# Filler matmuls in front of the last two weighted sums, and three quarters of tile 14's spread on VectorE

## The chip, the core and the metric

The kernel runs on one core of one Trainium2 chip. The metric is the device time in microseconds of one execution; the time before is the median of three runs, 365.45 us (365.2 to 366.1). A core has TensorE for matrix products, VectorE (DVE), ScalarE (ACT) and GpSimd (POOL) for elementwise work, and SyncE (SP), which here issues nearly all DMAs. Each engine takes its instructions in the order in which the program lists them; engines wait for each other by semaphores.

## The reference

One step of decoding for a batch of 8, with a gate `g` per row between attention and a small MLP:

```
g = sigmoid(sum(x * gate_w))                      # x: 8 x 576
q = x @ wq                                        # 32 heads of 128, 16 key/value heads
p = softmax(q . k * 128**-0.5)                    # the last 2048 positions of each cache
a = (p . v) @ wo                                  # wo: 4096 x 576
b = gelu(layernorm(x) @ w1 + b1) @ w2 + b2        # w1: 576 x 4608
out = g * a + (1 - g) * b
```

Everything is bf16. The key and value caches, 64 MB each in the part used, are nearly all of the 154 MB that are read.

## The kernel before, in words

The caches are cut into 16 K tiles and 16 V tiles of 4 MB, each for 32 pairs of batch row and head and a quarter of the positions. They stream through four slots of the arena (`RAW`), one DMA each, in the order K0 K1 V0 K2 V1 ... K15 V14 V15, then the bias b2, two pieces of w2 (`M` 0), the four blocks of wo (`W`) and the last three pieces of w2 (`M` 1). A DMA is issued by SyncE as soon as what used its slot is done; V14's slot takes the last block of wo and the last pieces of w2, so those wait for the weighted sum of tile 14.

For each tile n:

- VectorE transposes the K tile in four parts into the KT area (`tr`, L693), TensorE makes the scores (`qk`, L711, of which all but the first of four matmuls keep the loaded weights and are recorded in the helper at L175).
- VectorE takes the running maximum (`mx`, L644), ScalarE the exponentials (`exp`, L650) into P, VectorE transposes P (`pt`, L668).
- The P tile is spread into a block layout, a quarter (32 partitions x 2048) per instruction (`qrx`, L743 on VectorE and GpSimd, L742 on ScalarE). `px_engs` (L615) names the engine of each quarter: GpSimd two and ScalarE two, for tiles 0 to 13; one GpSimd, one ScalarE, two VectorE for tile 14; one ScalarE, three VectorE for tile 15.
- TensorE makes the weighted sum of V (`pv`, 64 matmuls of 128x256). Sums 0 to 14 are looped: two matmuls from L756, five rounds of twelve with register addresses (helper at L186), two more. Sum 15 is unrolled in two parts of 48 and 16 (`pva`, `pv`).
- VectorE adds the sum to the group's result (`o`, L792 and L794).

The block layout holds zeros between its blocks. Tiles 0 to 14 use the area `PX`, cleared once at the start (`ptx0`, L606). Tile 15 uses the KT area, which GpSimd clears by a memset of 128x4096 fp32 (`ktx0`, L726) after the last score matmuls; the spreads of tile 15 wait for it.

After sum 15, VectorE, GpSimd and TensorE bring the result into place (L794, L797, L800, L802, L805), ScalarE and VectorE into bf16 columns (L808, L809), and TensorE adds up the output: bias and w2 blocks, then wo (`proj0` to `proj3`), then the last w2 blocks, all at L580. Between the wo blocks and the last w2 blocks stand fillers (`keep_warm`, L814): matmuls of zeros that nobody reads, five (`warm0`) before `proj3`, five (`warm1`) after it. The first of a group is recorded at L819, the others at L175.

The order on each engine is no queue of the chip: a planner (`_Plan.schedule`, L62) places each operation by an assumed cost, a priority, its dependences (`deps`) and an order (`after`). Only `deps` become semaphore waits; `after` merely keeps an operation from being placed before another has been. Before, `ktx0` stands `after` the GpSimd quarter of tile 14 (L747), and the maximum of tile 15 `after` tile 14's VectorE quarters (L748).

Of the kernel before, what the change touches and what calls it, by code (L numbers as in the profile page):

```python
# [170 lines left out]
ARENA_BASE = 16512  # L171
# [21 lines left out]
def build_kernel(nc, A_x, A_k_cache, A_v_cache, A_wq, A_wo, B_x, B_w1, B_b1, B_w2, B_b2, gate_w, out):  # L193
# [10 lines left out]
    NL = 4 * NG  # L204
# [17 lines left out]
    with ExitStack() as es:  # L222
# [365 lines left out]
        for vi in range(NL):  # L588
            stream.append(("V", vi))
            if vi + 2 < NL:  # L590
                stream.append(("K", vi + 2))
        HEAD, BODY, TAIL = 2, 12, 2
        ROUNDS = (64 - HEAD - TAIL) // BODY
        assert HEAD and TAIL and HEAD + ROUNDS * BODY + TAIL == 64
        held_regs = []

        def regs():
# [14 lines left out]
        grp_done, acc_done = {}, {}  # L612
        mask_done, mx_done = {}, {}
        grp_first, sums = {}, {}
        px_engs = [("pool", "pool", "act", "act")] * (NL - 2) + [("pool", "act", "dve", "dve"), ("act", "dve", "dve", "dve")]  # L615

        def take_slot():
            n = n_slot[0]
# [109 lines left out]
        def v_item(n):  # L728
            s, d = load_item(A_v_cache, "dv", n)
            g, i = divmod(n, 4)  # L730
            if n == NL - 1:
                spread(n)
            ob_ = BK_OS[n % 2]
            px_at = aoffs("KT") if n == NL - 1 else PX
            px_free = [o_kz] if n == NL - 1 else [pv_done.get(n - 1), o_px0]
            px_done[n] = []
            for c in range(4):
                def fn(e, c=c):
                    dst = bass.AP(arena, offset=32 * c * AST + px_at + 32 * c, ap=[[AST, 32], [128, 64], [1, 32]])
                    src = bass.AP(arena, offset=32 * c * AST + aoffs("PT") + 2048 * (n % 2), ap=[[AST, 32], [32, 64], [1, 32]])  # L740
                    if px_engs[n][c] == "act":
                        return e.activation(out=dst, in_=src, func=ACTF.Copy)  # L742
                    return e.tensor_copy(dst, src)  # L743
                px_done[n].append(add(px_engs[n][c], fn, deps=[pt_done[n]] + px_free, name="qrx%d_%d" % (n, c), cost={"act": 1.8, "dve": 0.8, "pool": 2.4}[px_engs[n][c]], prio=5))

            if n == NL - 2:
                o_kz.after.append(px_done[n][0])  # L747
                mx_done[n + 1].after.extend(op for op in px_done[n] if op.eng == "dve")  # L748

            def pv_part(a, b):  # L750
                def fn(e):
                    mm = None
                    for k in range(a, b):
                        lhsT = bass.AP(arena, offset=px_at + 128 * k, ap=[[AST, 128], [1, 128]])
                        rhs = bass.AP(arena, offset=aoffs("RAW") + s * DE + 128 * k, ap=[[AST, 128], [SE, 2], [1, 128]])
                        mm = e.matmul(ps[:, ob_, 0:256], lhsT, rhs, start=(k == 0), stop=True, skip_group_check=True)  # L756
                    return mm
                return fn

            def pv_fn(e):  # L760
                pv_part(0, HEAD)(e)
                l, r = regs()
                e.reg_mov(l[0], ARENA_BASE + 2 * (PX + 128 * HEAD) + 254)
                e.reg_mov(r[0], ARENA_BASE + 2 * (aoffs("RAW") + s * DE + 128 * HEAD))
                with e.Fori(0, ROUNDS):
                    for i in range(BODY):
                        if i % 3 == 0:
                            if i:
                                e.reg_add(l[0], l[0], 768)
                                e.reg_add(r[0], r[0], 768)  # L770
                            for k in range(1, min(3, BODY - i)):
                                e.reg_add(l[k], l[0], 256 * k)
                                e.reg_add(r[k], r[0], 256 * k)
                        reg_matmul(nc, e, ps[:, ob_, 0:256], l[i % 3], [[AST, 128], [1, 128]], r[i % 3], [[AST, 128], [SE, 2], [1, 128]])
                    step = 256 * (BODY - (BODY - 1) // 3 * 3)
                    e.reg_add(l[0], l[0], step)
                    e.reg_add(r[0], r[0], step)
                return pv_part(64 - TAIL, 64)(e)
            deps = [d, o_u] + px_done[n] + [o_done.get(n - 2)]
            after = pv_hist[-1:] + [qk_unit.get(n + 1)]  # L780
            if n < NL - 1:
                pv = add("pe", pv_fn, deps=deps, name="pv%d" % n, cost=8.2, after=after)
            else:
                pva = add("pe", pv_part(0, 48), deps=deps, name="pv%da" % n, cost=5.4, after=after)
                sums[g].after.append(pva)
                pv = add("pe", pv_part(48, 64), deps=deps, name="pv%d" % n, cost=1.8, after=[sums[g]])
            pv_hist.append(pv)
            pv_done[n] = pv
            slot_free[s] = [pv]
            al = sm[:, n, 3:4]  # L790
            if i == 0:
                o_done[n] = add("dve", lambda e: e.tensor_copy(Oc, ps[:, ob_, 0:256]), deps=[pv, acc_done.get(g - 1)], name="o%d" % n, cost=0.4, prio=6)  # L792
            else:
                o_done[n] = add("dve", lambda e: e.scalar_tensor_tensor(out=Oc, in0=Oc, scalar=al, in1=ps[:, ob_, 0:256], op0=ALU.mult, op1=ALU.add), deps=[pv, al_done[n], o_done[n - 1]], name="o%d" % n, cost=0.5, prio=6)  # L794
            if i == 3:
                vmv = vm.rearrange("p (r d) -> p r d", r=2)
                vmul = add("dve", lambda e: e.scalar_tensor_tensor(out=vmv, in0=Oc.rearrange("p (r d) -> p r d", r=2), scalar=sg[:, g, 4:5],  # L797
                                                                   in1=bass.AP(arena_f, offset=foffs("maskrh"), ap=[[AST // 2, 128], [1, 2], [0, 128]]), op0=ALU.mult, op1=ALU.mult),
                           deps=[o_done[n], o_maskrh, o_hf] + grp_done[g], name="vmul%d" % g, cost=0.5, prio=6)
                acc_done[g] = add("dve", lambda e: e.tensor_reduce(out=EV, in_=vm.rearrange("p (r d) -> p d r", r=2), axis=AXL.X, op=ALU.add),  # L800
                                  deps=[vmul, us_done.get(g - 1)], name="acc%d" % g, cost=0.6, prio=6)
                ew = add("pool", lambda e: e.tensor_tensor(out=EW, in0=bass.AP(arena_f, offset=foffs("EV"), ap=[[AST // 2, 128], [0, 2], [1, 128]]),  # L802
                                                           in1=bass.AP(arena_f, offset=foffs("maskhd"), ap=[[AST // 2, 128], [1, 2], [0, 128]]), op=ALU.mult),
                         deps=[acc_done[g], o_maskhd, us_done.get(g - 1)], name="ew%d" % g, cost=0.6, prio=6)
                us_done[g] = add("pe", lambda e: e.matmul(ps[:, BK_S, 256:512], selv[:, 6 - 2 * g:134 - 2 * g], EW.rearrange("p h d -> p (h d)"), start=(g == 0), stop=True, skip_group_check=True),  # L805
                                 deps=[ew, o_u] + o_selv, name="us%d" % g, cost=0.7, prio=6)
            if n == NL - 1:
                oev = add("act", lambda e: e.activation(out=on, in_=ps[:, BK_S, 256:512], func=ACTF.Copy, scale=gcol), deps=[us_done[NG - 1], o_gcol], name="oev", cost=0.45, prio=9)  # L808
                o_T.append(add("dve", lambda e: e.transpose(bass.AP(arena, offset=aoffs("oT"), ap=[[AST, 128], [1, 256]]),  # L809
                                                            bass.AP(arena, offset=aoffs("on"), ap=[[AST, 128], [1, WOR], [WOR, 32]])), deps=[oev], name="oT", cost=0.6, prio=9))  # L810

        us_done, o_T = {}, []

        def keep_warm(name, n, after):  # L814
            def fn(e):
                mm = None
                for k in range(n):
                    args = (ps[:, k % 4, :], zeros_bf, maskR)
                    mm = e.matmul(*args, start=True, stop=True, skip_group_check=True) if k == 0 else held_matmul(nc, e, *args, start=True, stop=True, skip=True)  # L819
                return mm  # L820
            return add("pe", fn, deps=[ex_done[NL - 1], o_z, o_mR], name=name, cost=0.22 * n, after=after)

        def wo_all(_):
            def place(s, at, i):
# [6 lines left out]
                return AccGroup("proj%d" % i, [(oT[:, j, i, :], dj[:, j, :]) for j in range(WOR)], o_T + [d], cost=1.0, prio=1).op  # L831
            s = take_slot()
            done = [place(s, WO_CH * D * i, i) for i in range(3)]
            warm = keep_warm("warm0", 5, done[2:])
            slot_free[s] = done
            s = take_slot()
            done = [place(s, 0, 3)]
            done[0].after.append(warm)
            o_m2.append(keep_warm("warm1", 5, done))
            m2_at.append((s, WO_CH * D))  # L840
            slot_free[s] = done

# [104 lines left out]
```

## Time and profile before

| what | value |
|---|---|
| median of 3 runs (lowest, highest) | 365.45 us (365.2, 366.1) |
| the profiled execution's own time | 365.17 us |
| its span, first to last instruction | 363.9 us |
| TensorE, VectorE, ScalarE, GpSimd busy | 76%, 70%, 36%, 22% of the span |
| DMA | 154.47 MB, mean 424 GB/s |
| granted TensorE clock, mean | 0.93 |

The span is what the trace covers; the profiled execution took 1.3 us more. Times in the trace are counted from the span's start. "Granted clock" is the share of TensorE's full clock that it was given. A row of the timeline gives start and length, engine, line, operation, what is written and read and, in brackets, how long the engine was idle before and what ended that. TensorE has two rows, PE for matmuls and PEld for loads of weights. Since a line may be that of a helper, matmuls of several operations share L175 and L186.

### The profile page before, as it was taken

The page shows a single profiled execution, that of the slowest core. Times are in us where ns is not written, and L with a number is a line of the kernel's source. Part 1 is how long each engine was busy: PE and PEld are TensorE (multiplying, and loading weights), DVE is VectorE, ACT ScalarE, POOL GpSimd, SP SyncE. Part 2 cuts the span into 40 slices and gives each one's busy share as a digit, 9 for nine tenths or more (in the row PEclk, how much of TensorE's full clock was granted, in tenths as well). Part 3 has the DMA queues.
Part 4 walks back from the last instruction along what each step waited for, and adds up shares of the span by engine and source line. Part 5 has one row for each costly group of instructions (what it writes and reads, how often), then busy time and mean ns, then how long its engine had stood idle before and what let it go on. Part 6 is the DMA issues. An engine that isn't in the chain of part 4 may idle for free.

```text
span 363.9 us, 4246 instructions
## 1 busy us (share of the span) xinstructions
PE 277.4 (76%) x1818; PEld 126.9 (35%) x1381; DVE 254.9 (70%) x195; ACT 131.6 (36%) x117; POOL 78.8 (22%) x77
## 2 busy tenths in 40 slices
PE   0356464999897958996978769786868789975997
PEld 0110000345171704361434316251606043612863
DVE  0722978797978596949496878767685969398520
ACT  1012106274544442634343334444444417303400
POOL 9124001230414040402212040404040404006000
PEclk9976596999998998999899989999999879998999
DMA  8999999999999999999999999999999999999995
GB/s 348 433 439 402 461 403 458 407 457 418 447 420 443 421 443 425 434 430 432 436 432 436 432 430 432 443 421 447 418 447 416 450 414 451 414 450 413 420 428 226
DMA packets 6579, 154.47 MB, mean 424 GB/s; under 512 B 764, under 2 KB 932, under 8 KB 1320
## 3 DMA queue, kind: packets, MB, share of 16 engines
q1 hardware_dynamic: 6512, 154.29, 98.5%
q8 instruction: 7, 0.11, 0.1%
q10 hardware_dynamic: 56, 0.03, 0.0%
q14 instruction: 4, 0.03, 0.0%
HBM read 154.31 MB, written 0.01 MB: 424 GB/s over the span
## 4 chain that ended last, share of the span: by engine, by line
DMA 45%; DVE 35%; PE 13%; issue 4%; ACT 2%; POOL 0%; ACTq 0%
DMA arena<-in_A_k_cache_dram 43%; DVE arena L693 20%; DVE arena L668 5%; PE ps L175 4%; PE ps L186 2%; PE ps L756 2%; DMA arena<-in_gate_w_dram 2%; PE ps L580 2%; DVE arena L644 2%; DVE arena L797 1%; PE ps L502 1%; DVE arena L794 1%; DVE arena L743 1%; PE ps L711 1%; DVE arena L563 1%
## 5 line engine op out<-in xcount | busy, mean ns | idle before, releaser
L693 DVE STREAM_TRANSPOSE arena<-arena 128x2048 f32<-128x2048 f32 x64 | 145.0, 2288 | 28.4 <-DMA arena<-in_A_k_cache_dram 26.8
L175 PE MATMUL ps<-arena 128*128 128x512 bf16 (+2 forms) x446 | 126.8, 432 | 11.6 <-DVE arena L693 8.3
L743 POOL COPY arena<-arena 32x2048 bf16<-32x2048 bf16 x29 | 55.1, 1902 | 227.1 <-DVE arena L668 212.2
L186 PE MATMUL ps<-arena 128*128 x900 | 102.3, 275 | 0.0
L186 PEld LDWEIGHTS ps<-arena 128*128 x900 | 88.9, 99 | 11.3 <-issue 0.3
L711 PE MATMUL ps<-arena 128*128 128x512 bf16 x121 | 50.5, 417 | 50.1 <-DVE arena L693 43.4
L742 ACT ACTIVATE arena<-arena 32x2048 bf16<-32x2048 bf16 x30 | 57.2, 1906 | 70.5 <-DVE arena L668 67.8
L650 ACT ACTIVATE arena<-ps,arena 128x2048 bf16<-128x2048 f32 x16 | 31.5, 1967 | 107.6 <-DVE arena L648 74.7
L711 PEld LDWEIGHTS ps<-arena 128*128 128x128 bf16 x128 | 13.2, 103 | 162.5 <-DVE arena L693 104.7
L644 DVE TENSOR_REDUCE arena<-ps 128x1 f32<-128x2048 f32 x16 | 36.7, 2292 | 32.8 <-PE ps L175 32.8
L668 DVE STREAM_TRANSPOSE arena<-arena 128x2048 bf16<-128x2048 bf16 x16 | 36.4, 2274 | 2.1 <-ACT arena L650 2.1
L654 ACT ACTIVATE ps<-arena 128x2048 f32<-128x2048 f32 x15 | 28.1, 1872 | 0.1
L756 PE MATMUL ps<-arena 128*128 128x256 bf16 x124 | 19.0, 275 | 3.8 <-DVE arena L743 3.7
L756 PEld LDWEIGHTS ps<-arena 128*128 128x128 bf16 x124 | 12.0, 99 | 17.0 <-issue 14.0
L453 PE MATMUL ps<-arena 8*128 8x8 bf16 x8 | 0.6, 171 | 14.8 <-DVE arena L427 9.6
L558 DVE TENSOR_TENSOR arena<-arena 128x1152 f32<-128x1152 f32 x1 | 1.4, 1358 | 11.4 <-ACT arena L556 11.4
L580 PE MATMUL ps<-arena 128*8 128x288 bf16 (+1 forms) x140 | 9.3, 286 | 0.0
L637 POOL COPY arena<-arena 32x128 bf16<-32x128 bf16 x16 | 4.6, 287 | 15.3 <-ACT arena L537 7.7
L580 PEld LDWEIGHTS ps<-arena 128*8 128x8 bf16 (+1 forms) x140 | 5.8, 86 | 4.9 <-issue 1.9
L427 DVE COPY arena<-arena 8x64 bf16<-8x64 bf16 x2 | 0.3, 190 | 9.2 <-DMA arena<-in_gate_w_dram 9.2
L794 DVE SCALAR_TENSOR_TENSOR arena<-arena,ps 128x256 f32<-128x256 f32 x12 | 5.4, 447 | 1.4 <-PE ps L756 1.4
L890 DVE CAST arena<-ps 8x288 bf16<-8x288 f32 x1 | 0.4, 445 | 8.4 <-PE ps L580 8.4
(104 smaller groups left out, 99.0 us busy)
## 6 DMA issues: line engine op xcount, KB each, us to landing
arena<-in_A_k_cache_dram SPq DMA_DIRECT2D x16, 4096.0 KB, 27.1
arena<-in_A_v_cache_dram SPq DMA_DIRECT2D x16, 4096.0 KB, 26.9
arena<-in_B_w_dram SPq DMA_DIRECT2D x1, 4608.0 KB, 23.4
arena<-in_A_wo_dram SPq DMA_DIRECT2D x4, 1152.0 KB, 22.5
arena<-in_A_wq_dram SPq DMA_DIRECT2D x1, 4096.0 KB, 13.0
arena<-in_B_w_dram SPq DMA_DIRECT2D x2, 1728.0 KB, 24.3
arena<-in_B_w_dram SPq DMA_DIRECT2D x1, 1152.0 KB, 17.4
arena<-in_B_w_dram SPq DMA_DIRECT2D x1, 576.0 KB, 24.3
```

The source lines that it names most:

```text
L175: return e.add_instruction(mybir.InstMatmult(name=nc.get_next_instruction_name(), engine=mybir.EngineType.PE, ins=[e.lower_ap(rhs), e.lowe ...
L186: return e.add_instruction(mybir.InstMatmult(name=nc.get_next_instruction_name(), engine=mybir.EngineType.PE, ins=[operand(r, r_ap), opera ...
L580: ins = e.matmul(ps[32 * j:32 * j + 8, BK_ACC, 0:JN], lhsT, rhs[:, JN * j:JN * j + JN], start=False, stop=True, skip_group_check=True, til ...
L644: mx = mx_done[n] = add("dve", lambda e: e.tensor_reduce(out=k(n, MX), in_=ps[:, 0:4, :].rearrange("p a n -> p (a n)"), axis=AXL.X, op=ALU ...
L650: ex = add("act", lambda e: e.activation(out=Pm, in_=ps[:, 0:4, :].rearrange("p a n -> p (a n)"), func=ACTF.Exp, bias=k(n, NB), scale=SCAL ...
L654: mask_done[n + 1] = add("act", lambda e: e.activation(out=ps[:, 0:4, :].rearrange("p a (n c) -> p (a n) c", c=32), in_=bass.AP(arena_f, o ...
L668: pt_done[n] = add("dve", lambda e: e.transpose(bass.AP(arena, offset=aoffs("PT") + 2048 * (n % 2), ap=[[AST, 128], [1, 2048]]), Pm), deps ...
L693: tr = add("dve", (lambda rh=rh, hh=hh, kb=kb: lambda e: e.transpose(bass.AP(arena_f, offset=foffs("KT") + kb * 2048, ap=[[AST // 2, 128], ...
L711: mm = e.matmul(*args, start=False, stop=True, skip_group_check=True) if rc == 0 else held_matmul(nc, e, *args, stop=True, skip=True)
L742: return e.activation(out=dst, in_=src, func=ACTF.Copy)
L743: return e.tensor_copy(dst, src)
L756: mm = e.matmul(ps[:, ob_, 0:256], lhsT, rhs, start=(k == 0), stop=True, skip_group_check=True)
```

## The change

The spread of tile 14 moves from one GpSimd, one ScalarE, two VectorE quarters to one ScalarE, three VectorE. With it goes the order of `ktx0` behind the first quarter. The fillers `warm0` go, `warm1` has three matmuls where it had five; new fillers, ten before sum 14 and six before sum 15, stand behind whatever is ahead of those sums on TensorE. They write the PSUM bank of the sum that follows, after the sum of two tiles before has been read from it. Sums 0 to 13 are looped in ten rounds of six instead of five of twelve; sum 14 keeps twelve; the first 48 matmuls of sum 15 are looped in three rounds of fourteen. VectorE's addition of sum 14 is placed after VectorE's quarters of tile 15.

```diff
-        HEAD, BODY, TAIL = 2, 12, 2
-        ROUNDS = (64 - HEAD - TAIL) // BODY
-        assert HEAD and TAIL and HEAD + ROUNDS * BODY + TAIL == 64
+        HEAD = 2
...
-        px_engs = [("pool", "pool", "act", "act")] * (NL - 2) + [("pool", "act", "dve", "dve"), ("act", "dve", "dve", "dve")]
+        px_engs = [("pool", "pool", "act", "act")] * (NL - 2) + [("act", "dve", "dve", "dve"), ("act", "dve", "dve", "dve")]
...
             if n == NL - 2:
-                o_kz.after.append(px_done[n][0])
                 mx_done[n + 1].after.extend(op for op in px_done[n] if op.eng == "dve")
...
-            def pv_fn(e):
+            def pv_looped(e, end, tail, body):
                 pv_part(0, HEAD)(e)
...
-                with e.Fori(0, ROUNDS):
-                    for i in range(BODY):
+                with e.Fori(0, (end - HEAD - tail) // body):
+                    for i in range(body):
...
-                return pv_part(64 - TAIL, 64)(e)
+                return pv_part(end - tail, end)(e)
             deps = [d, o_u] + px_done[n] + [o_done.get(n - 2)]
             after = pv_hist[-1:] + [qk_unit.get(n + 1)]
+            if n >= NL - 2:
+                after.append(keep_warm("warm_pv%d" % n, (10, 6)[n - NL], after, (ob_,), [o_u, o_done[n - 2]]))
             if n < NL - 1:
-                pv = add("pe", pv_fn, deps=deps, name="pv%d" % n, cost=8.2, after=after)
+                pv = add("pe", lambda e: pv_looped(e, 64, 2, 6 if n < NL - 2 else 12), deps=deps, name="pv%d" % n, cost=8.2, after=after)
             else:
-                pva = add("pe", pv_part(0, 48), deps=deps, name="pv%da" % n, cost=5.4, after=after)
+                pva = add("pe", lambda e: pv_looped(e, 48, 4, 14), deps=deps, name="pv%da" % n, cost=5.4, after=after)
...
             al = sm[:, n, 3:4]
+            if n == NL - 1:
+                o_done[n - 1].after.extend(op for op in px_done[n] if op.eng == "dve")
...
-        def keep_warm(name, n, after):
+        def keep_warm(name, n, after, banks=(0, 1, 2, 3), deps=None):
             def fn(e):
                 mm = None
                 for k in range(n):
-                    args = (ps[:, k % 4, :], zeros_bf, maskR)
+                    args = (ps[:, banks[k % len(banks)], :], zeros_bf, maskR)
...
-            return add("pe", fn, deps=[ex_done[NL - 1], o_z, o_mR], name=name, cost=0.22 * n, after=after)
+            return add("pe", fn, deps=[o_z, o_mR] + (deps or [ex_done[NL - 1]]), name=name, cost=0.22 * n, after=after)
...
-            warm = keep_warm("warm0", 5, done[2:])
...
-            done[0].after.append(warm)
-            o_m2.append(keep_warm("warm1", 5, done))
+            o_m2.append(keep_warm("warm1", 3, done))
```

## The prediction, made before the changed kernel ran

> **What bounds the kernel now.** I read the page first. Its second part shows the DMA row at 9 tenths in every slice but the first and the last, and part 3 gives the hardware queue 98.5% of the 16 engines' span: 154 MB at 424 GB/s set the pace until about 10 us before the end. Then I read the chain of work that ended last, in order of time, to see where the pace passes to the engines.
>
> ```profile
> 293.03 25.41 DMA arena<-in_A_k_cache_dram
> 318.46 6.61 DVE arena L693 x3
> ...
> 327.71 2.23 DVE arena L668
> 329.97 0.68 DVE arena L743
> 330.65 0.03 issue
> 330.69 2.28 DVE arena L743
> 332.97 0.14 issue
> 333.10 0.41 PE ps L756 x2
> ```
>
> Columns are start, length, engine, line. The last K tile lands, VectorE transposes it (L693) and the P tile of sum 14 (L668), spreads two quarters of it (L743), and TensorE starts the weighted sum of tile 14 at 333.10. From there the chain is 8.9 us of that sum (333.10 to 342.00), sum 15 (342.21 to 349.5), the normalisation through VectorE, GpSimd and TensorE (to 352.4), and output blocks up to 361.97. The DMA issues page gives the other limit: the last three w2 pieces are issued from 342.40 to 343.4 and land 17.4 to 18.0 us later, the last at about 343.4 + 17.8 = 361.2. So at the end two limits lie less than 1 us apart: shortening the engines' chain can win at most some 0.6 us, and lengthening it costs in full.
>
> The two spreads above look alike and are not: 0.68 and 2.28 us for the same 32x2048 copy. The timeline shows what lay beside them.
>
> ```profile
> 329.97 2.98 DVE L743 COPY arena<-arena 32x2048 bf16<-32x2048 bf16 x2
> ...
> 330.00 2.40 POOL L743 COPY arena<-arena 32x2048 bf16<-32x2048 bf16 x1 [20.62 <-DVE arena L668]
> 332.52 3.88 POOL L726 MEMSET arena<- 128x4096 f32 x1
> ```
>
> GpSimd's copy ends at 332.40, VectorE's second copy 0.57 later: it stood still while GpSimd worked. In its turn GpSimd's copy took 2.40 where the other 28 took about 1.89: it waited for VectorE's first copy. The memset of L726 took 3.88; VectorE's copy ended 0.45 after the memset's start, and the rest is 3.43. Three copies with GpSimd idle, at 339.94, took 2.12 together.
>
> **Part 1: GpSimd no longer spreads a quarter of tile 14; VectorE takes three.** Alone this would be a gain: 2.12 instead of 3.00 us, so VectorE would be free at 332.1, not 332.97. But the same edit drops the ordering that put the memset of the KT area (L726, `ktx0`) behind that quarter on GpSimd's queue. What is left is its dependence on the last score matmuls, which end at 329.39 (L175, 328.55 + 0.84). GpSimd has nothing else queued, and in the memset of L606 it started 0.07 after TensorE's last matmul (32.80 to 32.87). So the memset starts at about 329.5, half a microsecond before VectorE's copies are ready at 329.97. What a VectorE instruction does when it meets a running memset is shown once:
>
> ```profile
> 32.87 3.51 POOL L606 MEMSET arena<- 128x4096 f32 x1 [5.24 <-PE ps L175]
> ...
> 35.40 1.59 DVE L559 TENSOR_SCALAR arena<-arena 128x1152 f32<-128x1152 f32 x1
> ```
>
> The memset ends at 36.38; the tensor_scalar begins inside it and ends at 36.99, 0.61 later, and took longer than the two-input operations of the same size (L558 and L560, 1.36). I read it as held back until the memset was over. Then the memset runs 329.5 to 333.0, the first copy ends 0.6 later, the other two take 1.4: VectorE is done at **335.0, not 332.97: 2.0 us late**. If nothing blocked, it would be 332.1 (0.9 early); these are the ends.
>
> The Trainium skill, SBUF — State Buffer, section Who interferes with whom, says that a VectorE copy in a two-port mode and a GpSimd instruction take one shared port pair by turns, whichever starts first keeping it for the whole instruction; the rows here agree (0.57 and 0.61 us after GpSimd's end). If the two shared the port instead, the copies would creep at the 0.68 : 2.28 ratio until 333.0 and end near 334.2, and the sum below would be 0.8 smaller.
>
> ScalarE's quarter (329.97, 1.91 us) is untouched. Behind the three copies on VectorE's queue stands the maximum of tile 15 (L644), and behind it the whole of tile 15: from 332.97 to the end of its spreads at 342.06 are 9.1 us, none of which changes (its spreads already were one on ScalarE and three on VectorE). So tile 15 is ready at 335.0 + 9.1 = **344.1**.
>
> **Part 2: fillers before the two sums.** Ten 128x512 matmuls on TensorE behind the last score unit: 0.225 each by the pace of L175 (0.84 for three, ends overlapping), 2.25 us, 329.45 to 331.7. They lie in TensorE's wait and cost nothing; their own waits, tile 12's evacuation at 307.79 and memsets of the start, are long over. What they should save is the clock. The granted clock in stretches of 3.41 us (columns: stretch, length, PE busy, PEld, DVE, ACT and POOL busy with counts, clock, DMA share, GB/s):
>
> ```profile
> 111.45:114.87 3.42, 1.44 (x7) 0.19 (x2) 3.42 (x5) 3.01 (x2) 2.95 (x2) 1.00 1.05 450
> 114.87:118.28 3.41, 3.18 (x10) 0.53 (x3) 2.14 (x4) 1.09 (x2) 0.82 (x1) 0.50 1.07 461
> 265.05:268.47 3.42, 1.50 (x7) 0.10 (x1) 3.42 (x2) 1.72 (x1) 1.69 (x1) 1.00 1.02 441
> 268.47:271.88 3.41, 2.19 (x10) 0.41 (x5) 3.13 (x5) 2.38 (x3) 2.08 (x2) 1.00 1.07 461
> 329.91:333.32 3.41, 0.22 (x2) 0.13 (x2) 3.31 (x4) 1.91 (x1) 3.20 (x2) 1.00 0.91 394
> 333.32:336.73 3.41, 3.41 (x18) 2.32 (x17) 2.12 (x2) 1.22 (x1) 3.09 (x1) 0.50 0.96 404
> ```
>
> With 1.44 of 3.42 us busy the next stretch runs at half clock, with 1.50 it does not: idle of some 1.95 us inside one stretch is the limit. Before, the gap was 3.7 us (329.39 to 333.10) and sum 14 paid: 8.9 us against 7.14 for sum 13 (312.26 to 319.40), 1.76. After, the copies hold sum 14 until 335.0 + 0.13 = 335.1, so the gap behind the fillers is 335.1 - 331.7 = 3.4 us. Wherever the stretches fall, one holds over 1.95 us of it except when it is split nearly in half (both parts between 1.45 and 1.95: 0.5 of 3.41, 15%). The loss is 1.7 when the whole half-clock stretch falls on the sum and about 0.9 when it begins in the gap; I take 1.5. Sum 14 then ends at 335.1 + 7.14 + 1.5 = 343.75 (342.25 without the loss).
>
> Six fillers before sum 15 are queued behind sum 14 and the small group matmul (0.2 us, as 342.00 to 342.21): 6 x 0.225 = 1.35. Sum 15 starts at 343.75 + 0.2 + 1.35 = **345.3**, later than its tile's 344.1: the fillers are now on the path. Before it started at 342.21, so **+3.1** (ends: +2.0, where tile 15 sets it, and +3.4).
>
> **Part 3: loops.** Sums 0 to 13 go in rounds of six, five more branches each. Sixty looped matmuls took 6.71 us (112 ns each) and 48 unrolled ones 5.40 (112.5), so the branches of today cost nothing seen. Upper end: one TensorE issue wait of 0.29 (333.49) per new branch, 1.5 us per sum; even then sum 13 would end at 320.9, against 320.83 for the next score unit, and K loads are issued 27 us before they land. I take 0. Sum 15's first 48 become looped: 0, at most 0.2 either way.
>
> **Part 4: fillers after.** `warm0` and two of `warm1` go.
>
> ```profile
> 352.37 4.58 PE L580 MATMUL ps<-arena 128*8 128x288 bf16 x72
> ...
> 358.06 1.15 PE L580 MATMUL ps<-arena 128*8 128x288 bf16 x16
> ...
> 359.14 0.39 PE L819 MATMUL ps<-arena 128*128 128x512 bf16 x1
> ...
> 360.33 1.64 PE L580 MATMUL ps<-arena 128*8 128x288 bf16 x24
> ```
>
> `warm0` took 356.95 to 358.06, 1.11; two of `warm1` are 0.45. **-1.56**, all on the path if TensorE is late. The block of wo rows behind it is issued at 342.03 and landed 14.9 later, 356.9; after the change its issue follows sum 14 to about 343.8, with 1.1 MB blocks issued at 327.4 still landing 22.5 us later in front of it, so the queue doesn't run dry.
>
> **Sum:** +3.1 - 1.56 = +1.55; TensorE ends at 363.5, past the landing at 361.2. The profiled execution took 365.17 (span 363.9 and 1.3 around it): 366.7. The median of the runs shown, 365.45, is 0.28 above it; I say **366.8**, range of this case 366.0 to 367.3.
>
> **Rivals.** (1) The copies are blocked but the clock holds: +2.0 - 1.56, 365.6 to 365.9. For it the 15% split; against it the gaps of 1.98 us (114.05) and 2.41 us (172.27) that cost the clock. The Trainium skill, TensorE: Matmul & The Clock Gate, section What's actually happening, asks for an idle window of about 3.4 us; by that this rival would be the rule, but 111.45:114.87 lost the clock with 1.44 us of work in it. 0.13. (2) On the other side: VectorE's copies aren't blocked, because the memset only writes or starts after them. Spreads end at 332.1, the gap is 0.5 us, the clock holds, sum 14 runs 332.2 to 339.35, tile 15 is ready at 341.2 and sum 15 starts 0.95 earlier; then wo (356.9) and the last w2 pieces (360.9 and 361.2) bind and TensorE ends near 361.4: -0.55, 364.6 to 364.9. No change is a start of sum 15 at 342.21 + 1.56 = 343.8: copies that end at 334.6 with the clock held (344.1 came from 335.0), at 333.5 with 1.5 lost. Before that point it isn't slower. Against it L559 and the 2.28 us copy. 0.11. (3) The new branches show after all, or the order of the end shifts: over 367.4, 0.04. The forecast: 0.72.
>
> A measurement of this kernel can't tell under 0.3% from no change. That puts the line at 366.55: of the forecast's 0.72 some 0.48 lie above it. Slower 0.52, the same 0.42, faster 0.06. Range 364.7 to 367.4.
>
> **What would show it.** The memset of L726 at 329.5, VectorE's three copies taking over 4 us from 329.97, sum 14 starting near 335.1 at half clock, six fillers directly in front of sum 15, no wait for w2 at the end. Wrong if the copies take 2.1 us beside the memset, or if the last matmuls wait for a DMA.

## The result, and the profile after

The changed kernel takes 366.51 us (median of 7 runs, 366.12 to 366.92); the kernel before took 365.22 beside it (365.19 to 366.1). The ratio of the two, as measured side by side, is 1.0029 with a 95% interval of 1.0017 to 1.0041 (the quotient of the medians would be 1.0035): slower than no change, by about 0.3%, and the interval doesn't say on which side of 0.3% it lies. The profiled execution took 366.66 us, its span is 365.4.

The timeline of the kernel after shows GpSimd's memset (now L724) and VectorE's three quarters of tile 14 (now L741):

```profile
329.47 3.51 POOL L724 MEMSET arena<- 128x4096 f32 x1 [20.05 <-PE ps L175]
...
329.99 4.96 DVE L741 COPY arena<-arena 32x2048 bf16<-32x2048 bf16 x3
```

The memset starts half a microsecond ahead and ends at 332.98. The three copies take 4.96 us; the same three for tile 15 take 2.12 (341.94). The chain of waits splits them and goes on to sum 15:

```profile
329.99 3.53 DVE arena L741
...
333.55 0.69 DVE arena L741
...
335.10 0.38 PE ps L753 x2
335.50 8.39 PE ps L186 x60
343.89 0.22 PE ps L753 x2
344.10 0.12 PE ps L672 x2
344.22 0.24 PE ps L821
344.46 1.08 PE ps L175 x5
345.54 0.22 PE ps L753 x2
```

Only the first copy is long (the next takes 0.69), and it ends at 333.52, 0.54 after the memset: nearly all of its work, 0.69 us where nothing is beside it, came after GpSimd had ended. Sum 14 starts at 335.10 and lasts until 344.1; a small matmul (L672) and the six fillers (L821, L175), to 345.4, stand on the chain, directly in front of sum 15. The stretches of 3.41 us around it (PE busy, PEld, DVE, ACT, POOL, granted clock, DMA share, GB/s):

```profile
333.01:336.42 3.41, 1.30 (x11) 0.97 (x12) 3.32 (x4) 0.00 (x0) 0.00 (x0) 1.00 0.99 426
336.42:339.83 3.41, 3.41 (x19) 2.35 (x17) 1.25 (x3) 2.29 (x4) 0.00 (x0) 0.50 0.97 415
339.83:343.24 3.41, 3.41 (x33) 3.05 (x32) 3.34 (x3) 1.64 (x2) 0.00 (x0) 1.00 0.99 422
```

The stretch with the end of the gap has 1.30 us of work, and all of the next runs at half clock: 19 matmuls where the one behind it has 33. The end, from the timeline:

```profile
355.55 5.56 PE L580 MATMUL ps<-arena 128*8 128x288 bf16 x88
...
361.79 1.64 PE L580 MATMUL ps<-arena 128*8 128x288 bf16 x24
```

The last wo block follows the others without a pause (88 matmuls in one row) and nothing waits for a DMA. TensorE ends at 363.43, 1.46 later than before.

### The profile page after: what moved, and what is told of

Its sections match the earlier page's. It is cut to its first block, busy times and chain, and to the rows that moved or that the text cites. A ratio compares the mean times of both kernels' runs of the same rounds, so it can differ in the third digit from the quotient of the medians.

```text
span 365.4 us, 4420 instructions
## 1 busy us (share of the span) xinstructions
PE 276.6 (76%) x1829; PEld 126.8 (35%) x1382; DVE 256.7 (70%) x196; ACT 131.6 (36%) x117; POOL 76.1 (21%) x76
## 4 chain that ended last, share of the span: by engine, by line
DMA 45%; DVE 35%; PE 13%; issue 4%; ACT 2%; POOL 0%; ACTq 0%
DMA arena<-in_A_k_cache_dram 43%; DVE arena L691 20%; DVE arena L666 5%; PE ps L175 4%; PE ps L186 4%; DMA arena<-in_gate_w_dram 2%; PE ps L580 2%; DVE arena L642 2%; DVE arena L799 1%; DVE arena L741 1%; PE ps L502 1%; DVE arena L796 1%; PE ps L753 1%; PE ps L709 1%; DVE arena L563 1%
## 5 line engine op out<-in xcount | busy, mean ns | idle before, releaser
L175 PE MATMUL ps<-arena 128*128 128x512 bf16 (+2 forms) x457 | 127.4, 427 | 11.7 <-DVE arena L691 8.7
L186 PE MATMUL ps<-arena 128*128 x942 | 107.1, 275 | 0.0
L186 PEld LDWEIGHTS ps<-arena 128*128 x942 | 92.8, 99 | 11.9 <-issue 0.3
L741 POOL COPY arena<-arena 32x2048 bf16<-32x2048 bf16 x28 | 52.8, 1885 | 206.7 <-DVE arena L666 205.9
L709 PE MATMUL ps<-arena 128*128 128x512 bf16 x120 | 49.3, 411 | 52.6 <-DVE arena L691 45.9
L648 ACT ACTIVATE arena<-ps,arena 128x2048 bf16<-128x2048 f32 x16 | 31.5, 1968 | 108.4 <-DVE arena L646 75.5
L709 PEld LDWEIGHTS ps<-arena 128*128 128x128 bf16 x128 | 13.1, 102 | 163.7 <-DVE arena L691 107.4
L642 DVE TENSOR_REDUCE arena<-ps 128x1 f32<-128x2048 f32 x16 | 36.7, 2291 | 31.8 <-PE ps L175 31.7
L753 PE MATMUL ps<-arena 128*128 128x256 bf16 x82 | 14.3, 272 | 3.5 <-DVE arena L741 3.5
L753 PEld LDWEIGHTS ps<-arena 128*128 128x128 bf16 x82 | 8.0, 99 | 18.6 <-issue 16.1
L635 POOL COPY arena<-arena 32x128 bf16<-32x128 bf16 x16 | 4.6, 287 | 15.3 <-ACT arena L537 7.7
L724 POOL MEMSET arena<- 128x4096 f32 x1 | 3.5, 3511 | 20.0 <-PE ps L175 20.0
L804 POOL TENSOR_TENSOR arena<-arena 128x256 f32<-128x256 f32 x4 | 2.5, 613 | 23.7 <-DVE arena L802 23.7
L741 DVE COPY arena<-arena 32x2048 bf16<-32x2048 bf16 x6 | 7.0, 1160 | 0.2
## 6 DMA issues: line engine op xcount, KB each, us to landing
arena<-in_B_w_dram SPq DMA_DIRECT2D x1, 1152.0 KB, 15.3
```

The costliest lines, as they stand in the source:

```text
L175: return e.add_instruction(mybir.InstMatmult(name=nc.get_next_instruction_name(), engine=mybir.EngineType.PE, ins=[e.lower_ap(rhs), e.lowe ...
L186: return e.add_instruction(mybir.InstMatmult(name=nc.get_next_instruction_name(), engine=mybir.EngineType.PE, ins=[operand(r, r_ap), opera ...
L642: mx = mx_done[n] = add("dve", lambda e: e.tensor_reduce(out=k(n, MX), in_=ps[:, 0:4, :].rearrange("p a n -> p (a n)"), axis=AXL.X, op=ALU ...
L648: ex = add("act", lambda e: e.activation(out=Pm, in_=ps[:, 0:4, :].rearrange("p a n -> p (a n)"), func=ACTF.Exp, bias=k(n, NB), scale=SCAL ...
L709: mm = e.matmul(*args, start=False, stop=True, skip_group_check=True) if rc == 0 else held_matmul(nc, e, *args, stop=True, skip=True)
```

## The experiments

Each ran beside the kernel before on the same chip, and its ratio is to that: e1 to e4 on one chip (median of before 365.49 us), e5 to e8 on another (365.21). In the traces of e1 to e5 the last K tile's transposes begin 0.3 to 0.4 us later than in the kernel before (318.8 to 318.9, not 318.5), so times inside those are compared from VectorE's first copy or from the start of sum 14, not from the span's start. A sum of V is timed from the start of its first matmul to the end of its last.

**e1: the memset behind the copies.**

```diff
             if n == NL - 2:
+                o_kz.deps.extend(px_done[n])
```

> The changed kernel, with one wait more: the memset of the KT area (ktx0) waits for all four quarters of tile 14's spread, so it can't run beside them. Theory (the running memset holds VectorE's copies back): the three copies take 2.1 us and end at 332.1, sum 14 starts at 332.2 after a gap of about 0.6 us on TensorE, at full clock, and ends near 339.4; tile 15 is ready at 341.2, sum 15 starts there, about 4.1 us before the changed kernel's 345.4; the last w2 pieces (landing near 361.2) then set the end: TensorE ends near 361.4, some 364.6 to 364.9 us, below both kernels. Rival (the copies are slow of themselves, or the time comes from loops and fillers): copies still 5 us, 366.5.

364.96 us, ratio 0.9981 (0.9972 to 0.9990): faster than both kernels. The timeline:

```profile
330.35 2.12 DVE L741 COPY arena<-arena 32x2048 bf16<-32x2048 bf16 x3
...
332.50 2.29 DVE L642 TENSOR_REDUCE arena<-ps 128x1 f32<-128x2048 f32 x1
...
332.61 0.38 PE L754 MATMUL ps<-arena 128*128 128x256 bf16 x2 [0.70 <-DVE arena L741]
332.67 3.51 POOL L724 MEMSET arena<- 128x4096 f32 x1 [23.22 <-DVE arena L741]
```

The same copies take 2.12 us once the memset isn't beside them. The memset now lies beside the maximum (L642), which takes its usual 2.29: not every VectorE instruction is held up. Sum 14 runs at full clock, from 332.61 to 339.95. The end has become the DMAs':

```profile
357.39 1.15 PE L580 MATMUL ps<-arena 128*8 128x288 bf16 x16 [0.73 <-DMA arena<-in_A_wo_dram]
...
360.17 1.72 PE L580 MATMUL ps<-arena 128*8 128x288 bf16 x24 [0.87 <-DMA arena<-in_B_w_dram]
```

TensorE waits 0.73 us for the last block of wo and 0.87 for w2, as it did for neither in the changed kernel. Sum 15 starts 11.4 us after VectorE's first copy (15.4 in the changed kernel, 12.2 before), and the fillers left out behind it would shorten the end by another 1.7 us; of these 2.5 us only 0.5 are left. An earlier issue doesn't bring these transfers sooner: the first of the last three w2 pieces lands at 359.8 in the kernel before (342.40 + 17.4) and at 359.8 in the changed kernel (344.51 + 15.3), and e1's, issued at 340.35, takes 19.8 (360.1, in a trace that runs 0.4 late). The rival, that the copies are slow of themselves, is out.

**e2: no fillers in front of sums 14 and 15.**

```diff
-            if n >= NL - 2:
-                after.append(keep_warm("warm_pv%d" % n, (10, 6)[n - NL], ...))
```

> The changed kernel without the fillers in front of sums 14 and 15. Theory (the ten lie in a wait and do not save the clock, the six lie on the path): gap on TensorE 5.7 us, sum 14 from 335.1 at half clock as in the changed kernel, ends near 344.1, sum 15 starts near 344.3 instead of 345.4: about 365.4, 1.1 less than the changed kernel. Rival (the ten fillers save part of the clock): sum 14 takes up to 1.7 us longer without them and the time stays at 366.5 or rises to 367.

365.94 us, ratio 1.0008 (0.9999 to 1.0017), 0.6 less than the changed kernel's median, 0.8 by the ratios, where 1.1 was expected. Sum 14 took 9.5 us (335.50 to 345.01), not 9.0: with a gap of 5.70 us the half clock covered two stretches, the first of them partly in the gap. So the ten do save something, 0.5 us (e8 has them alone); the six cost 1.3, and sum 15 starts 0.8 sooner after sum 14's start.

**e3: 22 fillers in front of sum 14.** `(10, 6)` becomes `(22, 6)`.

> The changed kernel with 22 fillers in front of sum 14 where it has ten; six in front of sum 15 as it has. Theory (a gap over some 1.95 us in one stretch costs the clock): 22 x 0.22 us fill TensorE until about 334.3, a gap of 0.8 is left, sum 14 runs at full clock, 335.1 to 342.3, the six fillers end near 343.9 and tile 15, ready at 344.1, sets the start of sum 15 at 344.2 instead of 345.4: about 365.3. Rival (only the late copies matter, the clock does not): sum 15 starts when it did, 366.5.

365.99 us, ratio 1.0015 (1.0005 to 1.0026). The copies still take 4.96, but the gap is 0.95, the clock stays at 1.00 and sum 14 takes 7.3 us (335.41 to 342.74). Sum 15 starts 9.1 us after sum 14's start instead of 10.3, when tile 15 is ready (342.25 + 2.12 = 344.37), as the theory has it. TensorE ends 32.4 us after VectorE's first copy (330.30 to 362.75), against 33.4 in the changed kernel: 1.0 us. The medians differ by 0.5 and the ratios by 0.0014 (0.5 us), half of the 1.2 that was expected; the intervals leave room for both sizes, so that the fillers save the clock is shown in the trace, and how much of it reaches the time is not.

**e4: the spread alone, in the kernel before.**

```diff
+        px_engs = ... + [("act", "dve", "dve", "dve"), ("act", "dve", "dve", "dve")]
-                o_kz.after.append(px_done[n][0])
+            if n == NL - 1:
+                o_done[n - 1].after.extend(op for op in px_done[n] if op.eng == "dve")
```

> The kernel before with the spread of tile 14 alone changed (one ScalarE, three VectorE; the memset no longer ordered behind a GpSimd quarter; VectorE's addition of sum 14 placed after tile 15's quarters): loops and fillers as before. Theory: copies end at 335.0, sum 14 from 335.1 at half clock to 344.0, sum 15 starts at 344.2, 2.0 later than before, and the ten fillers of the end stay: 367.2, the slowest of these. Rival (three copies on VectorE are a gain, and what costs the time in the changed kernel is its fillers or loops): 364.7 to 365.2.

367.61 us, ratio 1.0048 (1.0034 to 1.0062), the slowest, and 0.4 above what was expected. This part alone costs more than the whole change: the shorter end, worth 1.7 us (below), is missing here. Three stretches of this run:

```profile
330.34:333.75 3.41, 0.00 (x0) 0.00 (x0) 3.41 (x1) 1.91 (x1) 2.99 (x1) 1.00 1.07 461
333.75:337.16 3.41, 1.71 (x8) 0.98 (x9) 3.32 (x4) 0.00 (x0) 0.00 (x0) 0.50 0.87 372
337.16:340.58 3.42, 3.42 (x18) 2.42 (x17) 1.26 (x3) 2.63 (x4) 0.00 (x0) 0.50 1.00 421
```

The clock falls after an empty stretch, and the 1.71 us of work in the next didn't bring it back: the stretch behind that, busy throughout, still ran at 0.50. Sum 14 took 9.7 us (335.45 to 345.2), where 8.9 was expected.

**e5: rounds of twelve again.** `6 if n < NL - 2 else 12` becomes `12`.

> The changed kernel with sums 0 to 13 in five rounds of twelve again. Theory (the loops are beside the path: K tiles arrive at the pace of the DMA and TensorE waits for them): no change, 366.5 us beside the changed kernel's 366.5, and 1.003 of the kernel before. Rival (five more branches per sum cost up to 1.5 us each and part of it shows): faster by 0.5 us or more.

366.65 us, ratio 1.0031 (1.0019 to 1.0042), the changed kernel's 1.0029: the rounds of sums 0 to 13 change nothing that can be measured.

**e6: the kernel before, with the spread and the memset behind it.** The edits of e4 and of e1.

> The kernel before with the spread of tile 14 changed to one ScalarE and three VectorE quarters, and the memset of the KT area waiting for all four; VectorE's addition of sum 14 is placed after tile 15's quarters; loops and fillers as before. Theory (of the change only the spread can gain, 0.9 us, if the memset is kept off it, and the last DMAs cap it): copies end 2.1 us after they start, sum 14 starts 0.9 earlier and runs at half clock for a while, tile 15 and so sum 15 start 0.9 earlier, the end is set by the last landing: some 0.5 us under the kernel before, 364.9 to 365.1, like the changed kernel with its memset behind. Rival (the fillers in front of the sums are needed for that gain): 365.5, no change against before.

364.71 us, ratio 0.9981 (0.9972 to 0.9990), as e1. Here the gap in front of sum 14 is 2.86 us and the sum runs partly at half clock, 332.26 to 340.81; tile 15 is ready only at 341.22, so that costs nothing. The gain needs neither the new fillers nor the loops nor the shorter end: the time is capped where e1's is, by the last w2 pieces (TensorE waits 0.27 us for them, with all ten old fillers in place).

**e7: the memset in eight pieces.**

```diff
-        o_kz = add("pool", lambda e: e.memset(view("KT").bitcast(F32), 0.0), ...)
+            for i in range(8):
+                ins = e.memset(view("KT").bitcast(F32)[:, 512 * i:512 * i + 512], 0.0)
```

> The changed kernel with the memset of the KT area cut into eight instructions of 128x512. Theory (an instruction that has begun keeps the other engine out until it ends, and then the other may go): VectorE's copies pass between the pieces, each after at most one piece of 0.45 us: the three end about 3 us after they start instead of 5, sum 14 starts some 1.6 to 1.8 earlier and tile 15 too, and the last DMAs cap the gain: 365.0 to 365.2. Rival (GpSimd keeps VectorE out as long as it has instructions): the copies take 5 us, 366.5.

364.74 us, ratio 0.9985 (0.9975 to 0.9994). The timeline:

```profile
329.49 5.42 POOL L727 MEMSET arena<- 128x512 f32 x8 [20.23 <-PE ps L175]
330.01 3.02 DVE L746 COPY arena<-arena 32x2048 bf16<-32x2048 bf16 x3
```

The three copies, from the chain of waits:

```profile
330.01 1.00 DVE arena L746
...
331.05 0.98 DVE arena L746
...
332.06 0.99 DVE arena L746
```

The copies pass between the pieces: 3.02 us instead of 4.96, each 1.0 where one alone takes 0.69. Three of the eight pieces take 1.06 or 1.07 us (from 330.42, 331.43 and 332.44), the other five 0.52: each of the three stood still while a copy worked. The two take turns by instruction; GpSimd doesn't keep VectorE out for as long as it has work. Sum 15 starts 12.3 us after the first copy, as early as before the change, and the shorter end gives the gain, as far as the cap lets it: TensorE waits 0.87 us for w2, as in e1, and ends 31.6 us after the first copy (e1: 31.5), though its sum 15 starts 0.9 later than e1's. The time lies under the 365.0 to 365.2 that was expected, which had put the cap too high.

**e8: no fillers in front of sum 15, ten in front of sum 14.** `n >= NL - 2` becomes `n == NL - 2`.

> The changed kernel without the six fillers in front of sum 15; the ten in front of sum 14 stay. Theory (the ten cut the half clock from two stretches of 3.41 us to one, the six lie on the path): sum 14 takes 9.0 us as in the changed kernel, sum 15 starts when it has ended, near 344.3 instead of 345.4: 1.1 less, 365.4, and some 0.5 less than the kernel without any fillers in front. Rival (the ten save nothing): as the kernel without any, 365.9.

365.76 us, ratio 1.0010 (1.0000 to 1.0019). Sum 14 took 9.0 us (335.19 to 344.2) and sum 15 started at 344.29, 1.2 sooner after sum 14's start than in the changed kernel. That is the theory's place for the six. The time is 0.75 less than the changed kernel's and 0.9 less than that of e5, which ran on the same chip; expected were 1.1; beside e2 (1.0008) the ten's half microsecond isn't seen in the time, only in the traces.

## Why the prediction was right, point by point

- **The memset blocks the copies.** Forecast: memset at 329.5, copies done at 335.0. The trace: 329.47 and 334.97. e1 and e6 show the cause by taking the memset out from beside the copies, e7 by cutting it. The Trainium skill's rule (SBUF — State Buffer, Who interferes with whom), that one instruction keeps the pair of ports whole, agrees with these rows: the first copy ends 0.54 us after the memset, and e7's pieces and copies stand still for each other. The sharing that the prediction set beside it would have had the copies done at 334.2, and is out.
- **The clock is lost all the same.** Forecast: a gap of 3.4 us, sum 14 8.64 us long. The trace: 3.54 (331.56 to 335.10) and 9.0. The sum was 1.87 longer than sum 13, not 1.5. Of that 1.7 is the clock: the half-clock stretch began 1.3 us into the sum and fell on it whole, the case for which the prediction had 1.7. The other 0.2 is the start from a wait, which the prediction left out: at full clock in e1, e3 and e7 such a sum takes 7.3 us, not sum 13's 7.14. The rival that the clock holds was the wrong one here; e3, with the gap closed, is the kernel that it describes, and its ratio, 1.0015 of 365.22, makes 365.8, within the 365.6 to 365.9 given for it.
- **The six fillers come onto the path.** Forecast: sum 15 at 345.3, tile 15 ready at 344.1. The trace: 345.38 and 344.06. e8 shows the six by themselves. From the end of sum 14 to the start of sum 15 are 1.27 us, not the 0.2 + 1.35 of the prediction: the recorded ends of matmuls overlap the next starts, and six fillers take 1.30 from start to start.
- **The end.** Forecast -1.56; from the first wo matmul to TensorE's end it was 9.60 us before (352.37 to 361.97) and is 7.88 (355.55 to 363.43): -1.72.
- **The sum.** Forecast: TensorE's end at 363.5 and 366.7 us against this execution; measured 363.43 and 366.66. That it fits within 0.1 is partly luck: sum 14 ended 0.36 later than forecast, the way from there to sum 15 was 0.28 shorter and the end 0.16 shorter. The 0.1 us added for the median missed: 366.8 was forecast and 366.51 measured, because the median of before over more runs, 365.22, lies 0.05 above its profiled execution, not 0.28, and the changed kernel's lies 0.15 below its own. The line that the prediction drew between slower and the same was 366.55, with a chance of 0.52 above it; 366.51 lies just below, and the interval doesn't decide between the two.
- **The loops** (taken as 0): e5 for sums 0 to 13. The first 48 matmuls of sum 15, to the start of what follows them, took 5.24 us looped (345.38 to 350.62) and 5.23 unrolled (342.21 to 347.44).
- **The other side** (copies not blocked, 364.6 to 364.9, capped by the last w2 pieces): that time and its cap were right, within 0.1, for kernels in which they really aren't blocked, e1 (364.96) and e6 (364.71).
- **What was wrong** came later, in the expectations of e2 and e4: that a longer gap costs no more than a gap of 3.5 us. It cost 0.5 more in e2 and 0.7 in e4.

So the edit's own gain, 0.9 us on VectorE, was there, and was turned into a loss of 2.0 by the memset: it had stood behind GpSimd's quarter in GpSimd's queue, and that quarter is gone. The order (`after`) that was dropped with it would not have kept it back by itself: it would name ScalarE's quarter now, and `after` becomes no wait on the chip. It takes a dependence, as in e1 and e6. That is read from the planner; no run has the order alone.

## What to carry to other kernels

When work leaves a queue, look at what stood behind it: here a memset moved 3 us forward, into the one place where it blocked the engine on the critical path. Fillers are worth their place only while they end before the data of the work behind them is ready; count them against the gap that the changed kernel will have. And before shortening a chain, read what else ends at the same time: e1 took 2.5 us off it and gained 0.5, because the last transfers land when they did.

## What the runs showed of the hardware that was not expected

The clock falls by a sharp limit. The prediction had put it between 1.44 and 1.50 us of work in a stretch of 3.41 us, by one trace; all ten profiled executions agree. Their clock records have 861 stretches at full clock with a stretch behind them. All of the 85 that were followed by half clock had 1.45 us of TensorE's busy time or less; of the others only one had so little, and the next had 1.47 (e6, 266.90). At 1.45 itself both occur, e5 first, e4 second:

```profile
208.92:212.34 3.42, 1.45 (x7) 0.19 (x2) 3.38 (x3) 3.40 (x2) 3.36 (x2) 1.00 1.02 441
212.34:215.75 3.41, 0.73 (x4) 0.10 (x1) 3.11 (x3) 0.17 (x1) 0.80 (x2) 1.00 0.93 404
```

```profile
227.94:231.35 3.41, 1.45 (x7) 0.19 (x2) 3.41 (x4) 3.00 (x2) 2.94 (x2) 1.00 0.96 413
231.35:234.76 3.41, 3.19 (x9) 0.25 (x2) 1.66 (x1) 0.81 (x1) 0.83 (x1) 0.50 1.02 442
```

The stretch behind shows what the one in front has decided. So what keeps the clock is a share of work of some 43% in each stretch, not the absence of long gaps: in the kernel before, the gap of 2.41 us that ends at 172.27 cost the clock and the equal one that ends at 191.50 did not, since two stretches shared it (1.00 us of work in 169.48:172.89, 1.87 in 189.96:193.37).

The way back takes more busy time than staying does: in the ten traces no stretch at half clock with less than 2.3 us of it was followed by full clock, e4's 1.71 among them. What else decides it stays open: in seven traces a stretch near the start (from 25.8 to 28.0) was busy throughout and was still followed by half clock.
